# Fused attention and gelu layer on one core: the second layer's products of attentions 2 to 8 in 64x64 form, over four two-bank PSUM tiles

## The chip, the cores and the metric

The kernel runs on one core of a Trainium2 chip. TensorE (PE) does the matrix products and writes them into PSUM, eight banks of 512 float32 values per partition. ScalarE (ACT) does exponentials, gelu and copies, VectorE (DVE) elementwise work, reductions and 32x32 transposes, GpSimd (POOL) elementwise work in SBUF and some DMA issues, SyncE (SP) most DMA issues. Each engine runs its own list of instructions in order, and semaphores connect the lists. The metric is the device time of one execution in microseconds (us), lower is better.

## The reference

For each of 8 batches and 12 heads, with 448 positions and head size 64: q and k are normed by their root mean square and scaled by gains, the scores are a softmax of q times k transposed, and the result is multiplied by v. The heads are then joined to a matrix x of 3584 tokens by 768, and a two-layer network follows.

```python
q_n, k_n = (rmsnorm(q, g_q), rmsnorm(k, g_k))
scores = scale * np.matmul(q_n, k_n.transpose(0, 1, 3, 2))
attn = np.exp(scores - max); attn = attn / sum
x = matmul(attn, v) joined to [3584, 768]
h = x @ w_in                      # 768 x 2048
g = gelu_tanh(h)
out = g @ w_out                   # 2048 x 768
```

## The kernel before, in words

The work goes batch by batch, b = 0 to 7. A batch has an *attention*, a *first layer* (x times w_in, then gelu) and a *second layer* (g times w_out). The program's text is a hand-written order (`manual_schedule`): the instructions of an engine run in the order in which the Python code issues them.

**Attention** (`attention`, and `first_attention` for batch 0). The 12 heads are 3 groups c of 4. A group has 7 *units* t (line 333): four products of 64x64 weights with 448 columns each fill one two-bank PSUM tile `t` with the scores of 64 keys for four heads, and one ACT exponential (line 337) turns them into `ex`. DVE adds the `ex` of a group over t into `es` (`key_sums`, lines 353 to 359). Per group follow the *sums' product* (ones times `es`, four 64x64 products, line 384), the transposes, reciprocal and spreading of the sums on DVE (`turned`, `recips`, lines 393 to 404), the *value products* (v times `ex`, 28 products, line 384), and `quad_x` (line 417), which multiplies both into `xT`. Attention of batch b+1 is interleaved with the second layer of batch b, so that PE has work while ACT does the exponentials. "Attention 2" is that of b = 1.

**First layer**. For each of 16 blocks f of 128 gelu inputs, six 128x128 products of 448 columns go into one PSUM bank or one half of a two-bank tile. Blocks 0 to 3 go through `mm1_pair` (line 482), into two-bank tiles with one gelu of 896 columns (line 487); from block 4 on `mm1` (line 431) uses one bank from the pool `ps_m` and a gelu of 448 columns each (line 437).

**Second layer** (`mm2`, line 452). For a tile i of 128 tokens and a half of the 768 output columns, 16 products of 128x128 weights (a slice of g) with 384 columns of w_out add up in one bank of `ps_m`; then DVE (line 462) or ACT (line 460) copies them to `osb`, and when both halves are there two DMAs store the tile. Batches come in pairs with 7 tiles: 3 after the first, 4 after the second. `m2_parts` lists the products; `attention` gives them out in portions between groups of two or three units (`cuts`, `shares`). For b = 0 the list has all first halves ahead of all second halves (`order.sort`), and w_out itself is loaded in two halves of its columns by POOL's DMA queue (line 663). What is left after batch 7 runs at the end.

**PSUM** is 2 banks of `ps_m` and two-bank tiles that `pair` hands out in turn (`rounds`): two at first, three (`t0` to `t2`) once `start` is closed ahead of attention 2, which frees the banks of the first attention.

**Preparing q and k.** Loads (SP queue), squares (ACT or POOL), sums of squares (DVE reductions, line 170), norming (POOL), transposes by DMA and a gain on DVE (line 320) run ahead for later batches, at places given by the lists `m1`, `side`, `behind` and `ends`. In attention 2, POOL's squares of batch 2 wait for the gain of group 2 of batch 1 (line 673, `gpsimd_waits`), and six reductions on DVE follow them (`behind`, slot 4).

Of the kernel before, what the change touches and what calls it, by code (L numbers as in the profile page):

```python
# [17 lines left out]
def kernel(  # L18
# [43 lines left out]
    ps_m = ctx.enter_context(tc.tile_pool(name="ps_m", bufs=2, space=bass.MemoryType.PSUM))  # L62
    ps_t = ctx.enter_context(tc.tile_pool(name="ps_t", bufs=1, space=bass.MemoryType.PSUM))
    start = ctx.enter_context(ExitStack())
    ps_o = start.enter_context(tc.tile_pool(name="ps_o", bufs=1, space=bass.MemoryType.PSUM))
# [8 lines left out]
    def three():  # L74
        return len(rounds) == 3
# [164 lines left out]
    def rsqrt_last(b):  # L240
# [4 lines left out]
        if three():  # L245
            own, dst = pair("root")[:, 0], y
        else:
            own, dst = oall[0][:, S:], place(b, 1)
# [94 lines left out]
    def key_sums(b, c, t):  # L343

        n = added(b, c)
        if t > n or t == 0:
            return
        ex = exs[b, c]
        if t == 1:
            ess[b, c] = exq.tile([P, 2, S], BF16, tag="es", name="es")  # L350
        es = ess[b, c]
        if t == 1:
            nc.vector.tensor_add(es, ex[:, 0], ex[:, 1])
        elif t == n and n % 2 == 0 or c + 1 == NCH and t > 3:
            nc.vector.tensor_add(es, es, ex[:, t])  # L355
# [12 lines left out]
    def products(b, c, what, lo=0, hi=NT):  # L368

        if lo == 0 and three():  # L370
            o = oas["o", what] = pair("o")
            oas[what] = [o[:, r, :S] for r in range(2)]
        elif lo == 0:
            oas[what] = spare.pop() if spare else [o[:, :S] for o in oall]
        o = oas[what]
        es = [exs[b, c][:, t] for t in range(NT)]
        if not what and added(b, c):
            es[:added(b, c) + 1] = [ess[b, c]]
# [34 lines left out]
    def quad_x(b, c):  # L413
        if c == 0:
            xT[b] = xp.tile([128, HP, S], BF16, tag="xT", name="xT")
        if three():
# [25 lines left out]
    osbs, by_act = {}, []  # L442

    def mm2(b, i, half, f, lo, hi):

        end = b + 1 == B and i + 1 == 2 * S // 128
        if f == 0:
            osbs["ps"] = ps_m.tile([128, 512], F32, tag="mm", name="o")
            if lo == 0:
                osbs[i] = op.tile([128, d_model], F32, tag="osb", name="osb")  # L450
        o, osb = osbs["ps"][:, :hi - lo], osbs[i]
        nc.tensor.matmul(  # L452
            o, g[:, f, i * 128:(i + 1) * 128], wout[:, f, lo:hi],
            start=(f == 0), stop=(f == nf - 1),
        )
        if f + 1 < nf:
            return
        last = end and hi == d_model
        if b + 1 == B and (lo == 0 or end) or by_act:
            nc.scalar.copy(osb[:, lo:hi], o)  # L460
        else:
            nc.vector.tensor_copy(osb[:, lo:hi], o)  # L462
        if half == 0 and not end:
            return
        for j in range(2):
            col = i * 128 + j * R
            r = ((b // 2) * 2 + col // S) * R
            cols = slice(lo if end else 0, hi)
            eng = nc.scalar if last and j else nc.sync
            eng.dma_start(  # L470
                out_v[col % S // R, r:r + R, cols], osb[j * R:(j + 1) * R, cols]
            )

    def mm1_pair(i, cs=range(HP), b=0, js=range(2)):
# [11 lines left out]
        if cs[-1] == HP - 1 and js[-1] == 1:  # L486
            nc.scalar.activation(  # L487
                g[:, 2 * i:2 * i + 2, (b % 2) * S:(b % 2 + 1) * S], h[:, :, :S],
                AF.Gelu_apprx_tanh
            )  # L490

# [4 lines left out]
    def m2_parts(b):  # L496
        tiles = range(3) if b % 2 == 0 else range(3, 7)
        order = [(i, half) for i in tiles for half in range(2)]
        if b == 0:

            order.sort(key=lambda t: t[1])
        parts = [(i, half, half * HD, (half + 1) * HD) for i, half in order]
        if b + 1 == B:
            i, half, lo, hi = parts.pop()
            parts += [(i, half, lo, lo + HD // 2), (i, half, lo + HD // 2, hi)]
        return [
            lambda part=part, f=f: mm2(b, part[0], part[1], f, *part[2:])
            for part in parts for f in range(nf)
        ]

    def attention(b, m2, quota, side, behind, ends):


        units = [(c, t) for c in range(NCH) for t in range(NT)]
        cuts = (0, 3, 6, 9, 11, 13, 16, 18, 21)
        groups = [units[i:j] for i, j in zip(cuts, cuts[1:])]
        first, last, tail = (23, 16, 4) if b > 1 else (20, 14, 3)
        sums_at, x_at = {3: 0, 6: 1}, {4: 0}
        shares = (0, 13, 26, 35, 45, 58, 69) if b > 1 else (0, 13, 26, 34, 40, 53, 59)
        spread = quota - first - last - tail  # L520
        given = 0

        def upto(k):
            nonlocal given
            while given < k:
                m2.pop(0)()
                given += 1

        before = []
        for i, group in enumerate(groups):  # L530
            for fn in side.get(i, ()):
                fn()
            if b == 1 and i == 3:
                by_act.append(b)
            for c, t in group:
                unit(b, c, t)
            for c, t in before:
                key_sums(b, c, t)
            if i in x_at:
                products(b, x_at[i], 1)  # L540
                quad_x(b, x_at[i])
            elif i in sums_at:
                products(b, sums_at[i], 0)
                turned()
            if i == 0:
                n = first
            elif i < len(shares):
                n = spread * shares[i] // shares[-1] - spread * shares[i - 1] // shares[-1]
            else:
                n = last  # L550
            end = given + n

            upto(end - n // 2)
            if i in sums_at:
                recips()
            for c, t in group[:1 if i else 0]:
                key_sums(b, c, t)
            upto(end - n // 4)
            for c, t in group[1 if i else 0:-1]:
                key_sums(b, c, t)  # L560
            upto(end)
            before = group[-1:]
            for fn in behind.get(i, ()):
                fn()
        for fn in ends:
            fn()
        nc.scalar.preload_act_table_set(GELU_SET)

# [3 lines left out]
        c = NCH - 1  # L572
        products(b, c - 1, 1)
        for c, t in before:
            key_sums(b, c, t)
        quad_x(b, c - 1)
        products(b, c, 0)
        turned()
        products(b, c, 1)
        recips()  # L580

        by_act.append(b)
        upto(quota)
        mm1_pair(0, early, b)
        quad_x(b, c)
        mm1_pair(1, early, b)
        by_act.clear()

# [201 lines left out]
    m2 = []  # L790
    for b in range(B):
# [30 lines left out]
        elif b + 1 < B:  # L822

            m1.append((0, lambda: gpsimd_waits(ess[b, NCH - 1][:1, 0, :1])))
# [20 lines left out]
        for f in range(nf // 2 if b == 0 else nf):  # L845
# [8 lines left out]
            elif f > 3:  # L854
                mm1(b, f)
# [49 lines left out]
```

## Time and profile before

| | |
|---|---|
| times shown | 404.07 us median of 3 (403.87 to 404.14) |
| profiled execution: span of its instructions | 402.9 us |
| around the span (median less span) | 1.2 us |
| PE busy, share of the span | 394.0 us, 98% |
| ACT, DVE, POOL busy | 280.8, 257.7, 123.6 us |
| granted PE clock | 9 tenths or more in all 40 slices |
| attention 4 begins, attention 5 begins (PE) | 190.48 us, 237.43 us |

The profiled execution's own time is its span and about 1.2 us around it, so that its 402.9 us stand for the 404.07 us of the median. In a row of a timeline the columns are the start in us, the length in us, the engine, the source line, the operation with what it writes and reads, and the count of merged instructions; in square brackets stands the idle time ahead of it with what ended it. A row of the chain of work has the start, the length, the engine with the written tile and its line, and the count. In a row of the groups the two numbers behind the bar are the busy time in us and the mean of one in ns, then the idle time ahead of them.

### The profile page before, as it was taken

What the parts mean: (1) busy time and instruction counts of PE and PEld (TensorE: products, weight loads), DVE (VectorE), ACT (ScalarE), POOL (GpSimd) and SP (SyncE); (2) the same over time, 40 slices, a digit from 0 to 9 for tenths busy, and PEclk for the clock granted to TensorE, in tenths of its full rate; (3) what the DMA queues carried; (4) which work ended last, traced back from release to release, by engine and by line L of the source; (5) the groups of instructions that cost most, each with busy time, mean ns of one, the idle gap of its engine ahead of it and who ended that gap; (6) DMA issues with size and microseconds to landing.
All of it is one profiled execution on the core that took longest, in us unless ns stands there. A gap on an engine that the chain in (4) does not pass through costs nothing.

```text
span 402.9 us, 8097 instructions
## 1 busy us (share of the span) xinstructions
PE 394.0 (98%) x3319; PEld 209.7 (52%) x3319; DVE 257.7 (64%) x436; ACT 280.8 (70%) x382; POOL 123.6 (31%) x104
## 2 busy tenths in 40 slices
PE   7799999999999999999999999999999999999996
PEld 3365555555555555554555555555555545555564
DVE  5999868975796369845699257963698405990010
ACT  6995498778974887857975789748878359744301
POOL 4993407454007230183004540072301800000000
PEclk9999999999999999999999999999999999999999
DMA  8999996998415964169612948149513511210033
GB/s 287 297 224 207 199 210 215 243 242 222 91 39 116 245 110 131 41 167 279 114 41 63 251 69 217 40 86 266 77 42 78 117 24 39 51 47 23 2 78 80
DMA packets 65577, 54.07 MB, mean 134 GB/s; under 512 B 37380, under 2 KB 60548, under 8 KB 65540
## 3 DMA queue, kind: packets, MB, share of 16 engines
q1 hardware_dynamic: 53184, 41.48, 38.7%
q0 software_dynamic: 12128, 11.80, 19.0%
q8 instruction: 26, 0.43, 0.4%
q10 hardware_dynamic: 228, 0.28, 0.2%
q14 instruction: 11, 0.09, 0.1%
HBM read 45.61 MB, written 11.01 MB: 141 GB/s over the span
## 4 chain that ended last, share of the span: by engine, by line
PE 92%; ACT 4%; DMA 2%; POOL 1%; SPq 0%; DVE 0%; issue 0%
PE o L452 38%; PE h L431 24%; PE t L482 12%; PE t L333 9%; PE t L384 8%; ACT ex L337 4%; DMA rawq<-in_q_dram 2%; POOL g L161 1%; PE tp L291 0%; PE o L384 0%; SPq L626 0%; PE os L384 0%; DVE ss L170 0%; ACT lg L195 0%; SPq L121 0%
## 5 line engine op out<-in xcount | busy, mean ns | idle before, releaser
L337 ACT ACTIVATE ex<-t,shift 128x896 bf16<-128x896 f32 x168 | 157.4, 1006 | 21.7 <-PE t L333 19.3
L452 PE MATMUL o<-wout,g 128*128 128x384 bf16 (+1 forms) x912 | 156.8, 324 | 0.0
L452 PEld LDWEIGHTS <-g 128*128 128x128 bf16 x912 | 83.6, 98 | 67.8 <-issue 18.8
L431 PE MATMUL h<-xT,win 128*128 128x448 bf16 x516 | 99.1, 352 | 0.0
L170 DVE TENSOR_REDUCE ss<-sq 128x14 f32<-128x896 f32 (+3 forms) x45 | 44.3, 999 | 48.9 <-ACT sq L159 45.9
L431 PEld LDWEIGHTS <-win 128*128 128x128 bf16 x516 | 50.5, 98 | 47.1
L437 ACT ACTIVATE g<-h 128x448 bf16<-128x448 f32 x86 | 46.6, 543 | 28.2 <-PE h L431 23.1
L462 DVE COPY osb<-o 128x384 f32<-128x384 f32 x41 | 22.7, 553 | 52.8 <-PE o L452 50.8
L333 PE MATMUL t<-qT,kT 64*64 64x448 bf16 x672 | 47.0, 359 | 2.6 <-ACT lg L195 1.0
L482 PE MATMUL t<-xT,win 128*128 128x448 bf16 x252 | 49.5, 353 | 0.0
L673 POOL COPY mark<-es 1x1 bf16<-1x1 bf16 x6 | 1.1, 176 | 131.8 <-DVE es L355 124.6
L487 ACT ACTIVATE g<-t 128x896 bf16<-128x896 f32 x21 | 18.4, 915 | 32.9 <-PE t L482 32.9
L273 POOL TENSOR_TENSOR nrmq<-rawq,rinv 128x896 bf16<-128x896 f32 (+1 forms) x21 | 34.8, 1658 | 10.0 <-DVE o L236 6.4
L482 PEld LDWEIGHTS <-win 128*128 128x128 bf16 x252 | 24.5, 98 | 22.6 <-issue 0.4
L273 POOL TENSOR_TENSOR nrmk<-rawk,rinv 128x896 bf16<-128x896 f32 x20 | 33.6, 1680 | 0.0
L333 PEld LDWEIGHTS <-kT 64*64 64x64 bf16 x672 | 17.4, 105 | 27.4 <-issue 20.3
L384 PE MATMUL t<-ex,vb 64*64 64x448 bf16 x588 | 31.6, 350 | 0.0
L460 ACT COPY osb<-o 128x384 f32<-128x384 f32 (+1 forms) x16 | 7.3, 458 | 31.4 <-PE o L452 31.4
L404 DVE STREAM_TRANSPOSE rb<-rc 128x896 f32<-128x896 f32 (+1 forms) x25 | 26.8, 1073 | 0.8
L384 PEld LDWEIGHTS <-vb 64*64 64x64 bf16 x672 | 20.2, 107 | 12.0 <-issue 3.0
L358 DVE TENSOR_TENSOR e<-ex 128x896 bf16<-128x896 bf16 x33 | 20.0, 606 | 9.7 <-ACT ex L337 9.4
L393 DVE STREAM_TRANSPOSE st<-t 128x448 f32<-128x448 f32 x42 | 24.6, 624 | 1.0 <-PE t L384 0.9
(93 smaller groups left out, 296.2 us busy)
## 6 DMA issues: line engine op xcount, KB each, us to landing
out_dram<-osb SPq DMA_DIRECT2D x54, 192.0 KB, 2.7
rawq<-in_q_dram SPq DMA_DIRECT2D x23, 448.0 KB, 4.6
rawk<-in_k_dram SPq DMA_DIRECT2D x23, 448.0 KB, 5.8
vb<-in_v_dram POOLq DMA_DIRECT2D x6, 672.0 KB, 6.5
win<-in_moe_w_in_dram POOLq DMA_DIRECT2D x8, 384.0 KB, 10.4
wout<-in_moe_w_out_dram POOLq DMA_DIRECT2D x2, 1536.0 KB, 22.3
vb<-in_v_dram POOLq DMA_DIRECT2D x2, 448.0 KB, 17.9
vb<-in_v_dram POOLq DMA_DIRECT2D x2, 224.0 KB, 12.1
```

Source lines behind the costliest of these rows:

```text
L170: nc.vector.reduce_sum(sss[b][:, seat(b, c), "qk".index(n), hs, ts], squares(b, c, n, hs, ts), axis=AX.X)
L273: eng.tensor_mul(nrms[n, b, c][:, ts].rearrange("p t a d -> p a t d"), raws[n, b, c][:, :, ts], root[:, :, ts].to_broadcast([P, 2, m, D]),)
L333: nc.tensor.matmul(sc[r * R:(r + 1) * R, a, :S], kT[rs, c, t, r], qT[b][rs, c, :, r], start=True, stop=True,)
L337: nc.scalar.activation(ex[:, t], sc[:, :, :S], AF.Exp, scale=scale, bias=shift)
L384: nc.tensor.matmul(o[r][a * D:(a + 1) * D], vb[b % 2][rs, 2 * c + a, i] if what else ones[rs], es[i][rs, a], start=(i == 0), stop=(i == n ...
L393: nc.vector.transpose(st[:, r].rearrange("p a b -> p (a b)"), oas[0][r])
L404: nc.vector.transpose(oas["rb"][:, rs].rearrange("p r s -> p (r s)"), rc.to_broadcast([128, (rs.stop - rs.start) * m, 32]),)
L431: nc.tensor.matmul(h[:, :S], win[:, c, f * 128:(f + 1) * 128], xT[b][:, c], start=(c == 0), stop=(c == HP - 1),)
L437: nc.scalar.activation(g[:, f, (b % 2) * S:(b % 2 + 1) * S], h[:, :S], AF.Gelu_apprx_tanh)
L452: nc.tensor.matmul(o, g[:, f, i * 128:(i + 1) * 128], wout[:, f, lo:hi], start=(f == 0), stop=(f == nf - 1),)
L462: nc.vector.tensor_copy(osb[:, lo:hi], o)
L482: nc.tensor.matmul(h[:, j, :S], win[:, c, f * 128:(f + 1) * 128], xT[b][:, c], start=(c == 0), stop=(c == HP - 1),)
```

## The change

It replaces `mm2`, `m2_parts` and the giving out by portions.

- In attentions 2 to 8 the second layer goes by whole tiles of 128 tokens (`quartered`): a *step* is four products of 64x64 weights with 384 columns, one for each pair of a half r of the 128 inner values of block f and a half a of the tokens. Half r goes to bank `(r + turn) % 2`, that is to that half of the output columns. 16 steps make turn 0, 16 more turn 1, with the banks changed over. Ahead of turn 1 PE waits (`follows`) for the last product of turn 0. The tile sits in one two-bank PSUM tile, which is taken out of the rotation for that time, and one copy of 768 columns brings it out: DVE for the first tile of an attention, ACT for the other two.
- The order in an attention is written out as a list: "u" a unit, a number so many steps, "s" a group's sums' product with `turned` and `recips`, "x" its value products with `quad_x`. Units stand single between 4 to 6 steps. Three tiles (96 steps) go into each attention; from attention 3 on, one more half tile is done in the old form by `whole` behind it.
- `ps_m` is released with `start`, and two more two-bank tiles take those banks: `rounds` has four (`t0` to `t3`). The first layer from block 4 on uses `mm1_pair` with gelus of 896 columns, but the last pair has its two gelus apart.
- `key_sums` adds pairs: `es` has room for two, and the sums of a group are two additions of 1792 columns, a fold of 896 and one more of 896, where there were six of 896.
- The last four tiles (`final`) take a two-bank tile each, both halves in the old form, with a copy for each half.

```diff
+    def quartered(b, i, eng):
+        o = rounds.pop(0)
+        for turn in range(2):
+            for f in range(nf):
+                if turn and f == 0:
+                    follows(mm)
+                for r in range(2):
+                    rs, half = slice(r * D, (r + 1) * D), (r + turn) % 2
+                    for a in range(2):
+                        at = i * 128 + a * R
+                        mm = nc.tensor.matmul(
+                            o[a * R:(a + 1) * R, half, :HD], g[rs, f, at:at + R],
+                            wout[rs, f, half * HD:(half + 1) * HD],
...
+                if turn and f + 1 == nf:
+                    rounds.append(o)
...
+        for what in ("u", 16, "uuu", 6, "u", 5, "u", 5,
+                     4, "u", 5, "u", 5, "u", 2, "us", 5, "u", 5, "u", 5, "u", 1,
+                     5, "uxu", 4, "u", 4, "u", 3, "us", 2, "u", 4, "u", 4, "u", 6, "x", "sx"):
...
+                    elif made > 2:
+                        key_sums(b, *done[-3])
...
+        if b > 1:
+            half, i = b % 2, 6
+            o = pair("o")[:, half, :HD]
+            whole(i, o, half * HD, (half + 1) * HD)
...
-        if t == 1:
-            nc.vector.tensor_add(es, ex[:, 0], ex[:, 1])
-        elif t == n and n % 2 == 0 or c + 1 == NCH and t > 3:
-            nc.vector.tensor_add(es, es, ex[:, t])
-        elif t % 2:
-            e2 = exq.tile([P, 2, S], BF16, tag="e2", name="e2")
-            nc.vector.tensor_add(e2, ex[:, t - 1], ex[:, t])
-            nc.vector.tensor_add(es, es, e2)
+        if t == 3:
+            nc.vector.tensor_add(es, ex[:, :2], ex[:, 2:4])
+        elif t == 5:
+            nc.vector.tensor_add(es, es, ex[:, 4:6])
+            nc.vector.tensor_add(es[:, 0], es[:, 0], es[:, 1])
+        elif t == 6:
+            nc.vector.tensor_add(es[:, 0], es[:, 0], ex[:, 6])
...
-                mm1(b, f)
+            elif f + 1 == nf:
+                mm1_pair(f // 2, b=b, js=(0,))
+                mm1_pair(f // 2, b=b, js=(1,))
+            elif f % 2 and f > 3:
+                mm1_pair(f // 2, b=b)
...
+            for i in (2, 3):
+                rounds.insert(0, ps_x.tile([128, 2, 512], F32, tag=f"t{i}", name=f"t{i}"))
```

More of the change, by code (lines that the diff above doesn't have):

```diff
@@ L441 @@
     out_v = out.rearrange("(r t) d -> t r d", t=NT)
[L442 to L465, printed above, removed]
+    osbs = {}
@@ L466, in mm2, with osb_of, store @@
+    def osb_of(i):
+        osbs[i] = op.tile([128, d_model], F32, tag="osb", name="osb")
+    def store(b, i, lo=0, hi=d_model, engs=(nc.sync, nc.sync)):
+        for j, eng in enumerate(engs):
             col = i * 128 + j * R
             r = ((b // 2) * 2 + col // S) * R
-            cols = slice(lo if end else 0, hi)
-            eng = nc.scalar if last and j else nc.sync
             eng.dma_start(
-                out_v[col % S // R, r:r + R, cols], osb[j * R:(j + 1) * R, cols]
+                out_v[col % S // R, r:r + R, lo:hi], osbs[i][j * R:(j + 1) * R, lo:hi]
@@ L494 @@
     even, odd = early[::2], early[1::2]
[L496 to L509, printed above, removed]
@@ L511, in attention @@
-    def attention(b, m2, quota, side, behind, ends):
-        units = [(c, t) for c in range(NCH) for t in range(NT)]
-        cuts = (0, 3, 6, 9, 11, 13, 16, 18, 21)
[L516 to L565, printed above, removed]
```

145 lines of the change are left out of this document (111 added, 34 removed).

## The prediction

> **What bounds the kernel now.** I read the page's busy shares and the chain that ended last, then that chain in order of time, then the timelines of PE, ACT, DVE and POOL, and the groups of instructions for durations.
>
> ```profile
> PE 394.0 (98%) x3319; PEld 209.7 (52%) x3319; DVE 257.7 (64%) x436; ACT 280.8 (70%) x382; POOL 123.6 (31%) x104
> PE 92%; ACT 4%; DMA 2%; POOL 1%; SPq 0%; DVE 0%; issue 0%
> ```
> ```profile
> 190.55 0.69 PE t L333 x12
> 191.24 3.84 PE o L452 x23
> ...
> 203.67 1.32 PE t L384 x28
> ...
> 215.62 2.97 PE t L384 x60
> ...
> 219.34 4.54 PE t L482 x24
> 223.88 13.62 PE h L431 x72
> 237.50 0.69 PE t L333 x12
> ...
> 378.35 20.85 PE o L452 x144
> ```
>
> PE is the bound, and in attentions 2 to 8 it never waits. The rows give its prices. The last row is 128 full slots (32 of its 144 products have half the columns): 20.85 / 128 = 0.163 us for 384 columns. 13.62 / 72 = 0.189 us for 448 columns. 28 small products are 7 sets of four: 1.32 / 7 = 0.189 us a set, so four 64x64 products side by side take what one 128x128 product takes. A period is 237.50 - 190.55 = 46.95 us. Its work is 45 sets and 96 first-layer products at 0.189 and 112 second-layer products at 0.163, together 44.9. The missing 2.05 us is changes of array form: between 190.55 and 219.34 PE goes nine times into 64x64 products and back, so 0.23 each. From single rows: 0.69 - 3 x 0.189 = 0.12 going in, 3.84 - 23 x 0.163 = 0.09 coming out, 0.21. I take 0.22.
>
> **The change part by part.** All sums are against the profiled execution: span 402.9 us, about 1.2 us around it, together the median of 404.07.
>
> *Removed: changes of form.* The list in `attention` leaves one round trip of nine. 8 x 0.22 x 7 attentions = 12.3 us of PE time. A step is four products of 384 columns; its nearest row is the 0.189 set of 448 columns, and with the columns it comes to 0.163 (bounds: 0.163, and 0.189 if something other than columns set that row; I take 0.163, because 0.189 equals the full-array price of 448 columns exactly). So the second layer itself costs what it did. Whether the 12.3 us come out depends on what is late next, and I find five places.
>
> *1. The second half of w_out.*
>
> ```profile
> L663 POOL DMA_DIRECT2D wout<-in_moe_w_out_dram x2: 1204/1213/1222, 26.8 to 32.0; - x2
> DMA to landing us min/median/max: 18.5/22.3/26.2
> ```
> ```profile
> 50.79 0.76 PE L333 MATMUL t<-qT,kT 64*64 64x448 bf16 x12
> 51.48 3.42 PE L452 MATMUL o<-wout,g 128*128 128x384 bf16 x20
> ...
> 61.35 1.47 PE L452 MATMUL o<-wout,g 128*128 128x384 bf16 x8
> ...
> 78.32 4.70 PE L482 MATMUL t<-xT,win 128*128 128x448 bf16 x24
> ```
>
> The second half is issued at 32.0 and lands 26.2 later, at 58.2. Before, 48 products use first halves only, and the 49th (in the row at 61.35) comes after the landing. After, the first step already has r = 1 writing the second half of the columns: PE stands from its third small product of attention 2 until 58.2, with all units behind it in its list. Against 51.48 that is **6.7 us**. The DMAs ahead of it are unchanged, so its bounds are narrow, 6 to 7.5. (The first unit also waits for the transposes' last copy, whose banks its tile now has; that lies inside the same wait.)
>
> *2. The rest of attention 2.*
>
> ```profile
> 60.18 0.45 DVE L320 TENSOR_SCALAR kT<-kT,gcols 128x896 bf16<-128x896 bf16 x1
> ...
> 64.81 1.09 DVE L417 TENSOR_TENSOR xT<-t,rb 128x896 bf16<-128x896 f32 x1 [0.58 <-PE t L384]
> 65.82 4.17 DVE L170 TENSOR_REDUCE ss<-sq 128x14 f32<-128x896 f32 x6
> ```
> ```profile
> 61.59 1.68 POOL L161 TENSOR_TENSOR sq<-rawq 128x896 f32<-128x896 f32 x1 [0.72 <-DMA rawq<-in_q_dram]
> ...
> 66.65 1.82 POOL L161 TENSOR_TENSOR sq<-rawk 128x448 f32<-128x448 f32 x2
> ```
> ```profile
> rawk<-in_k_dram SPq DMA_DIRECT2D x23, 448.0 KB, 5.8
> ```
>
> Before, `quad_x` of group 0 (64.81) stands ahead of the six reductions. In the new list `behind` is emitted with unit 14, ahead of that `quad_x`. The reductions need POOL's squares, which begin after the gain and take 68.5 - 61.6 = 6.9 us. After, the sums of group 0 are ready about 10.3 us after restart, 68.5, the gain ends at 68.9, the squares at 76.0, the reductions at 76.6, `quad_x` at 77.7. Unit 17 needs the PSUM tile that this `quad_x` reads, and PE is there at about 76.0: a wait of 1.7, or of 2.8 if the loads of groups 1 and 2 (issued at about 67.2 behind two stores, 5.8 to land) hold the squares up by 1.1. I take 2.8 (bounds 1.7 and 3.6). PE's own work from 58.2 is 25.3 us (52 sets, 96 steps, less what ran before); with waits of 0.85 at the first sums' product and 1.2 at the third (reckoned as in 3) and 0.2 in all elsewhere it is 30.35. Before, 78.32 - 51.48 = 26.84: **+3.5 us**, the removed 1.8 of changes included.
>
> *3. Attentions 3 to 8: DVE's sums are late.*
>
> ```profile
> 190.48 0.76 PE L333 MATMUL t<-qT,kT 64*64 64x448 bf16 x12
> ...
> 201.24 0.36 PE L384 MATMUL t<-es,ones 64*64 64x448 bf16 x4
> ...
> 216.90 0.36 PE L384 MATMUL t<-es,ones 64*64 64x448 bf16 x4
> ```
> ```profile
> 192.44 2.80 ACT L337 ACTIVATE ex<-t,shift 128x896 bf16<-128x896 f32 x3
> ```
> ```profile
> 199.67 0.62 DVE L355 TENSOR_TENSOR es<-es,ex 128x896 bf16<-128x896 bf16 x1
> ...
> 201.79 1.17 DVE L393 STREAM_TRANSPOSE st<-t 128x448 f32<-128x448 f32 x2
> 202.99 0.33 DVE L399 RECIPROCAL rc<-st 128x28 f32<-128x28 f32 x1
> 203.36 1.11 DVE L404 STREAM_TRANSPOSE rb<-rc 128x896 f32<-128x896 f32 x1
> ...
> 214.75 2.08 DVE L355 TENSOR_TENSOR es<-es,ex 128x896 bf16<-128x896 bf16 x3
> ```
> ```profile
> L355 DVE TENSOR_TENSOR es<-es,ex 128x896 bf16<-128x896 bf16 x33 | 20.6, 623 | 2.8
> L462 DVE COPY osb<-o 128x384 f32<-128x384 f32 x41 | 22.7, 553 | 52.8 <-PE o L452 50.8 <-DMA out_dram<-osb 1.9
> ```
>
> Before, the first sums end at 200.29, 0.95 ahead of their product; the third end at 216.83, 0.07 ahead of theirs. There is no room at the third. New sizes have no row. The copy of 768 columns: an estimate of 0.95, from 0.553 for 384 and 1.09 for 896. An addition of 1792 columns: 1.08, taking 0.15 of 0.623 as fixed, as the copy's line through those points gives; bounds 0.62 (no dearer than 896) and 1.25 (twice). Dependent DVE rows stand 0.04 apart (202.99 + 0.33 to 203.36), independent ones overlap by 0.08.
>
> With T the first unit: exponentials begin at T + 1.96 and come every 0.9 (2.80 less 1.0 for one, over two). Units 2 to 4 follow 16 steps, so exponentials 2, 3, 4 begin at 3.2, 4.1, 5.0, and the fourth ends at 6.0. DVE: addition to 7.1, copy of the first tile to 8.0, addition to 9.0, fold to 9.65, addition to 10.3. PE is at the first sums' product after 10 units and 48 steps, 9.7: **wait 0.65**. Then 0.19 + 21 steps + 4 units and 0.1 bring value products 0 to 14.8 to 16.15, and 4 units and 11 steps the second sums' product to 18.7. DVE: transposes, reciprocal, spread until 13.5, addition to 14.5, `quad_x` 16.35 to 17.4, addition to 18.45, fold to 19.1, addition to 19.75: **wait 1.1**. Then 0.19, 3 units, 16 steps and value products 1 bring the third to 24.5; DVE has the second spread until 22.9, then two additions, fold and addition until 26.35: **wait 1.9**. From 26.4 follow 0.19 + 1.32 + 0.1 + 16 x 0.163: the first layer begins at T + 30.6. Before it was 219.34 - 190.55 = 28.8. So **+1.8 us** in each of six attentions: waits of 3.65 against 1.8 removed.
>
> *4. The last gelus of a first layer.*
>
> ```profile
> L437 ACT ACTIVATE g<-h 128x448 bf16<-128x448 f32 x86 | 46.6, 543 | 28.2 <-PE h L431 23.1
> L431 PE MATMUL h<-xT,win 128*128 128x448 bf16 x516 | 99.1, 352 | 0.0
> L487 ACT ACTIVATE g<-t 128x896 bf16<-128x896 f32 x21 | 18.4, 915 | 32.9 <-PE t L482 32.9
> L460 ACT COPY osb<-o 128x384 f32<-128x384 f32 (+1 forms) x16 | 7.3, 458 | 31.4 <-PE o L452 31.4
> ```
>
> In the built order the second half of the last pair waits for the gelu of the first half, which reads the same two-bank tile. A result is there 0.352 - 0.189 = 0.163 after its slot; gelu 0.543; two hand-overs at 0.045: **0.8 us**, seven times, 5.6. Before, two banks in turn hid it.
>
> *5. `final`.* In the same way the second half of each of the last four tiles waits for the copy of the first: 0.163 + 0.458 + 0.09 = 0.7, **2.85 us** in all.
>
> *At nothing:* `follows` (two sets or more stand between the turns, 0.38 against 0.163 + 0.05 until the product is done; without that cover 0.2 x 21 = 4); ACT's copies of 768 columns (0.78 by 0.458 and the slope of 0.915 and 0.543; ACT has 21 x 0.9 + 1.6 + 0.7 = 21.2 us in an attention of 30); pairs of gelus in the first layer (0.915 against 12 products, 2.27); stores, as many and as large.
>
> Sum: 6.7 + 3.5 + 6 x 1.8 + 5.6 + 2.85 = 29.5; 402.9 + 29.5 + 1.2 = **433.6 us**.
>
> **The rivals.**
>
> *A. PE works past a waiting product (faster).* If products further down PE's list ran while one waits, only PE's own work would count: 404.07 - 12.3 = 391.8. The waits found above come to 29.5 + 12.3 = 41.8 us; the change is faster only if over 29.5 of them, 7 tenths, are filled so. Against it:
>
> ```profile
> 28.38 0.38 PE L333 MATMUL t<-qT,kT 64*64 64x448 bf16 x4 [0.52 <-ACT ex L337]
> ```
>
> PE stood 0.52 us for an exponential though later products were in its list. Chance 0.04.
>
> *B. Small products are bound by issue.* 28 products with their loads in 1.32 us are 23.6 ns an instruction. If that is a floor, a step takes 0.189: at most 0.026 x 672 = 17.5 us more; waits for DVE swallow about half: 442. The exact equality with the full-array price speaks against it. Chance 0.11.
>
> *C. Weight loads lie bare.*
>
> ```profile
> L384 PEld LDWEIGHTS <-vb 64*64 64x64 bf16 x672 | 20.2, 107 | 12.0 <-issue 3.0
> ```
>
> If each step paid its 0.107 load, 672 x 0.107 = 72: about 506. The 0.189 set contains such loads and shows none of it. Chance 0.02. [...]
>
> *D. Wide additions are cheap.* At 0.62 the waits of 3 fall from 3.65 to about 1.5 and some of attention 2 goes: 420. The row of 623 ns is for half the columns, so this needs columns to cost nothing. Chance 0.07.
>
> **How the numbers follow.** Forecast 0.76, with a range of its own of 427 to 440 (place 2, the additions by 0.08 either way); A 0.04, B 0.11, C 0.02, D 0.07. 0.2% of the time is what a measurement can tell from no change. Faster 0.03 and same 0.01 are A; slower 0.96. The range of 423 to 443 has the forecast, most of B and the dear half of D, and leaves out A, C and the rest.
>
> **What would show it.** A gap on PE in attention 2 that ends near 58.2 by the second w_out load; periods of about 49.5 us; sums' products with waits of 0.65, 1.1 and 1.9 ended by DVE additions; 0.8 ahead of the last half pair, ended by a gelu; four gaps of 0.7 at the end; second-layer steps 0.163 apart. It is wrong if steps are 0.189 or more apart, if additions of 1792 columns are far from 1.08, or if a wait behind `follows` shows.

## The result, and the profile after

The changed kernel takes **440.5 us** (median of 4 runs, 439.65 to 441.2) against 404.07 us (4 runs, 403.87 to 404.14): a ratio of 1.090, with a 95% interval of 1.088 to 1.091. It is slower by 36 us. The prediction said 433.6, with 423 to 443 as its range and 427 to 440 as the forecast's own. The side and the range hold; the point is 6.9 us short.

From the page of the changed kernel: the busy shares and the chain that ended last by engine, which the prediction shows of before, and between them the granted PE clock in 40 slices, where before every slice had 9:

```profile
PE 389.8 (89%) x5335; PEld 236.5 (54%) x5335; DVE 240.4 (55%) x365; ACT 282.6 (64%) x357; POOL 123.4 (28%) x104
...
PEclk9999969999999999999999999999999999999999
...
PE 55%; DVE 17%; DMA 9%; ACT 7%; POOL 6%; issue 5%; SPq 0%; DVEq 0%; ACTq 0%; POOLq 0%
```

PE is busy for 4 us less than before, and its share falls from 98% to 89% of a longer span (438.6 us). The chain goes through PE for 55% where it was 92%: DVE, a DMA, ACT and POOL now release work that PE stands in front of. One slice of 40 has a lower clock, of which more below.

The view of waits on PE, of the changed kernel (engine, tile and line, then who ended the wait: us in total, times, longest):

```profile
PE t L386 <- DVE es L361: 21.6, 18, 1.9
PE t L485 <- DMA wout<-in_moe_w_out_dram: 7.0, 1, 7.0
PE t L509 <- ACT g L516: 4.4, 7, 0.6
PE t L460 <- ACT osb L606: 2.4, 4, 0.6
...
PE t L336 <- DVE xT L419: 1.4, 1, 1.4
...
PE t L336 <- DVE rawk L142: 0.9, 1, 0.9
```

The first five rows are the forecast's five places: DVE's sums 18 times (three in each of six attentions), the second half of w_out once, the last gelu seven times, `final` four times, and a unit in attention 2. Together they are 36.8 us of idle PE. The last row is the first unit of attention 2, of which more at the end of the part on the prediction. The view counts idle time only, from the end of the product ahead, which lies behind the end of that product's slot (0.35 us against 0.189 for 448 columns), so a start-to-start gap is 0.16 to 0.20 longer than its row in attention 4 (0.74 for 0.57, 2.09 for 1.93).

The timeline of PE in attention 4 of the changed kernel (the attention begins at 159.78 and the next at 210.00, a period of 50.22 where it was 46.95):

```profile
160.00 2.77 PE L485 MATMUL t<-wout,g 64*64 64x384 bf16 x64
162.60 0.74 PE L336 MATMUL t<-qT,kT 64*64 64x448 bf16 x12
...
170.24 0.38 PE L386 MATMUL t<-es,ones 64*64 64x448 bf16 x4 [0.57 <-DVE es L361]
...
179.90 0.38 PE L386 MATMUL t<-es,ones 64*64 64x448 bf16 x4 [1.09 <-DVE es L361]
...
186.70 0.38 PE L386 MATMUL t<-es,ones 64*64 64x448 bf16 x4 [1.93 <-DVE es L361]
...
190.95 17.19 PE L509 MATMUL t<-xT,win 128*128 128x448 bf16 x90
208.77 1.29 PE L509 MATMUL t<-xT,win 128*128 128x448 bf16 x6 [0.63 <-ACT g L516]
```

The first row answers rival B: 16 steps take 162.60 - 160.00 = 2.60 us, 0.1625 a step, which is the price of a 128x128 product of 384 columns. The second layer itself got no dearer. In brackets stand the waits for the three sums, and the last row is the half pair that waits for a gelu. As start-to-start gaps they are 0.74, 1.29, 2.09 and 0.80. Without these four gaps a period would be 45.30 us, 1.65 less than the 46.95 of before.

The DVE timeline of the same attention shows why the third is the longest:

```profile
181.98 1.11 DVE L406 STREAM_TRANSPOSE rb<-rc 128x896 f32<-128x896 f32 x1
183.02 1.05 DVE L356 TENSOR_TENSOR es<-ex 128x1792 bf16<-128x1792 bf16 x1
184.17 1.09 DVE L358 TENSOR_TENSOR es<-es,ex 128x1792 bf16<-128x1792 bf16 x1
185.29 0.62 DVE L359 TENSOR_TENSOR es<-es 128x896 bf16<-128x896 bf16 x1
186.02 0.62 DVE L361 TENSOR_TENSOR es<-es,ex 128x896 bf16<-128x896 bf16 x1
```

DVE is not idle here: the third group's four additions begin only as the second group's spread (L406) ends, at 183.1, and they end at 186.64. PE has been out of work since 184.8. DVE is busy for 55% of the span and is nevertheless what PE waits for.

The second half of w_out, in the PE timeline of the changed kernel, and the windows around its landing (busy us of PE, PEld, DVE, ACT and POOL with counts, the granted clock, the DMA share, GB/s):

```profile
50.81 0.55 PE L294 MATMUL tp<-ident,nrmk 128*128 128x128 bf16 x7
52.28 0.38 PE L336 MATMUL t<-qT,kT 64*64 64x448 bf16 x4 [0.92 <-DVE rawk L142]
52.47 0.35 PE L485 MATMUL t<-wout,g 64*64 64x384 bf16 x2
59.85 4.09 PE L485 MATMUL t<-wout,g 64*64 64x384 bf16 x62 [7.03 <-DMA wout<-in_moe_w_out_dram]
```
```profile
54.00:56.00 2.00, 0.00 (x0) 0.00 (x0) 0.00 (x0) 0.00 (x0) 0.00 (x0) 0.93 1.27 192
56.00:58.00 2.00, 0.00 (x0) 0.00 (x0) 0.00 (x0) 0.00 (x0) 0.00 (x0) 0.50 1.21 254
...
59.80:61.00 1.20, 1.15 (x16) 0.87 (x19) 0.00 (x0) 0.00 (x0) 0.00 (x0) 0.50 0.98 262
61.00:62.40 1.40, 1.40 (x24) 0.95 (x17) 0.00 (x0) 0.00 (x0) 0.00 (x0) 0.50 0.55 117
62.40:63.60 1.20, 1.20 (x33) 1.01 (x29) 0.00 (x0) 0.00 (x0) 0.00 (x0) 0.94 0.02 3
```

PE stands from its second small product until 59.85, as the forecast had it. What it did not have is the clock: while PE idled, the grant fell to 0.50, and it stayed there after the data had come. From the shares of the first and the last window it was at half from 55.7 to 62.5, so that the first 2.7 us of work ran at half speed. The 62 products are 15.5 steps, 2.52 us at 0.1625, and the next unit begins 3.77 us after their start, at 63.62, so the half clock lost 1.25 us.

Where the 35.7 us between the two spans lie: up to the first layer of attention 2, +12.2; the first layer of attention 2, +0.8; five periods (attentions 3 to 7) by 3.27, +16.4; the last attention with its layer and `final`, +6.4. The remaining 0.7 of the 36.4 is not in the kernels. The 1.2 us that were put around the span of before set one execution's span against the median of others; where time and span of one and the same execution are known, they are 2.0 us apart before (404.84 and 402.8) and 2.1 after (440.73 and 438.6).

### The profile page after: what moved, and what is told of

Read it like the earlier page. It is cut to its first block, busy times and chain, and to the rows that moved or that the text cites. A ratio compares the mean times of both kernels' runs of the same rounds, so it can differ in the third digit from the quotient of the medians.

```text
span 438.6 us, 12084 instructions
## 1 busy us (share of the span) xinstructions
PE 389.8 (89%) x5335; PEld 236.5 (54%) x5335; DVE 240.4 (55%) x365; ACT 282.6 (64%) x357; POOL 123.4 (28%) x104
## 4 chain that ended last, share of the span: by engine, by line
PE 55%; DVE 17%; DMA 9%; ACT 7%; POOL 6%; issue 5%; SPq 0%; DVEq 0%; ACTq 0%; POOLq 0%
PE t L509 29%; PE t L485 9%; PE t L460 9%; DMA wout<-in_moe_w_out_dram 6%; PE t L386 6%; ACT ex L340 5%; DVE es L358 5%; DVE es L359 3%; DMA rawq<-in_q_dram 3%; DVE es L361 3%; PE t L336 2%; POOL g L164 2%; DVE xT L419 2%; DVE st L395 2%; POOL sq L164 2%
## 5 line engine op out<-in xcount | busy, mean ns | idle before, releaser
L509 PE MATMUL t<-xT,win 128*128 128x448 bf16 x756 | 145.9, 352 | 4.4 <-ACT g L516 4.4
L485 PE MATMUL t<-wout,g 64*64 64x384 bf16 x2688 | 133.1, 325 | 7.0 <-DMA wout<-in_moe_w_out_dram 7.0
L516 ACT ACTIVATE g<-t 128x896 bf16<-128x896 f32 (+1 forms) x70 | 58.1, 842 | 73.2 <-PE t L509 73.2
L485 PEld LDWEIGHTS <-g 64*64 64x64 bf16 x2688 | 83.8, 108 | 36.3 <-issue 7.4
L336 PE MATMUL t<-qT,kT 64*64 64x448 bf16 x672 | 60.2, 352 | 5.0 <-DVE xT L419 1.4
L356 DVE TENSOR_TENSOR es<-ex 128x1792 bf16<-128x1792 bf16 x20 | 21.3, 1065 | 52.0 <-ACT ex L340 52.0
L460 PE MATMUL t<-wout,g 128*128 128x384 bf16 (+1 forms) x240 | 38.3, 315 | 2.4 <-ACT osb L606 2.4
L460 PEld LDWEIGHTS <-g 128*128 128x128 bf16 x240 | 22.5, 98 | 18.1 <-issue 5.5
L419 DVE TENSOR_TENSOR xT<-t,rb 128x896 bf16<-128x896 f32 x21 | 22.8, 1088 | 12.5 <-ACT ex L340 11.7
L406 DVE STREAM_TRANSPOSE rb<-rc 128x896 f32<-128x896 f32 (+1 forms) x25 | 26.8, 1073 | 0.8
L164 POOL TENSOR_TENSOR sq<-rawq 128x896 f32<-128x896 f32 (+1 forms) x9 | 13.6, 1511 | 38.1 <-DVE ss L173 35.0
```

The lines of the kernel that those rows point to most:

```text
L164: eng.tensor_mul(sq, raw, raw)
L336: nc.tensor.matmul(sc[r * R:(r + 1) * R, a, :S], kT[rs, c, t, r], qT[b][rs, c, :, r], start=True, stop=True,)
L419: nc.vector.tensor_mul(xT[b][:, 2 * c:2 * c + 2], oas["o", 1][:, :, :S], oas["rb"])
L460: nc.tensor.matmul(o, g[:, f, i * 128:(i + 1) * 128], wout[:, f, lo:hi], start=(f == 0), stop=(f == nf - 1),)
L485: mm = nc.tensor.matmul(o[a * R:(a + 1) * R, half, :HD], g[rs, f, at:at + R], wout[rs, f, half * HD:(half + 1) * HD], start=(turn == 0 and ...
L509: nc.tensor.matmul(h[:, j, :S], win[:, c, f * 128:(f + 1) * 128], xT[b][:, c], start=(c == 0), stop=(c == HP - 1),)
```

## The experiments

The theory was that PE's own work became cheaper by the changes of form, and that five places where PE now stands idle took that back and more. The rivals were that some of the idle time would return elsewhere as soon as it is taken away at one place, that the second layer in 64x64 is itself dear, and that the changes of form had cost nothing in the first place. The ratios below are to the kernel before on the same chip, with the 95% interval in brackets.

### One place at a time

**Attention 2 with its second layer in the old form** (places 1 and 2): its three tiles in 128x128, first halves of all tiles first, with the order of units that the kernel before has there.

```diff
...
+        if b == 1:
+            m2 = halved(b - 1, tiles)
...
+        early_list = ("uuu", 20, "uuu", 13, "uuu", 13, "uus", 8, "uux", 6, "uuu", 13, "uus", 6, "uuu", 17, "x", "sx")
-        for what in ("u", 16, "uuu", 6, ...
+        for what in early_list if b == 1 else ("u", 16, "uuu", 6, ...
```

> Attention 2 alone is put back: its second layer in 128x128 products, first halves of all tiles ahead of second halves, units in groups of two and three as before; all else as in the changed kernel. Theory (the second half of w_out holds PE up, and the DVE and POOL waits of that attention are a cause of their own): the wait of 7.0 us and the slow clock behind it (about 1.2) go, eight form changes (1.8) come back, the waits for reductions and sums stay: attention 2 from 57.3 to about 50.5, in all 433.5 us. Rival 1 (those other waits only follow from the late start): attention 2 back to 45.8, in all 429. Rival 2 (not w_out but the rotation of four tiles or the wide sums make attention 2 long): over 438.

Measured: 432.8 us, 1.070 [1.066, 1.074]. Attention 2 takes 50.24 us where it took 57.28, and the other periods stay at 50.22. The PE timeline has no wait for w_out any more, and shorter ones in its place:

```profile
72.55 1.52 PE L386 MATMUL t<-ex,ones 64*64 64x448 bf16 x28 [1.59 <-ACT osb L542]
...
81.02 0.38 PE L386 MATMUL t<-es,ones 64*64 64x448 bf16 x4 [0.86 <-DVE es L359]
```

The theory's number holds. Attention 2 is still 4.5 us longer than the 45.78 of before, and the gelu's wait (0.8) and these are most of it. The first row waits for ACT's copy of second-layer halves, which sit in one of the four rotating tiles where they used to have banks of their own; the second waits for DVE's sums. The granted clock is 1.00 throughout, so in these runs the half clock goes with the wait for w_out.

**The last pair of the first layer in two tiles** (place 4):

```diff
-        if cs[0] == 0 and js[0] == 0:
+        if cs[0] == 0 and (js[0] == 0 or len(js) == 1):
             hs1[i] = pair("hh")
```

> The two halves of the last first-layer pair go to two different two-bank tiles, so that the second need not wait for the gelu of the first. Theory: 0.80 us less in each of seven batches, 440.5 - 5.6 = 434.9 us, and the gap ahead of those six products is gone. Rival (the wait only moves: the first exponential of the next attention or the first unit's tile is late instead): 440 to 441.

Measured: 436.3 us, 1.079 [1.074, 1.083]. The first layer is one row again in the timeline:

```profile
190.76 18.32 PE L509 MATMUL t<-xT,win 128*128 128x448 bf16 x96
```

The periods are 49.43, shorter by the expected 0.79. The total fell by 4.2 and not by 5.6: in this run w_out landed at 60.0, and the clock was at half until 64.3 (up to 62.5 in the changed kernel), which took back about 0.8, and the unit that waits for the first `quad_x` stood 1.9 us in the view of waits instead of 1.4.

**The second halves of the last four tiles in another tile** (place 5):

```diff
-                    po = (pair("o")[:, 0] if lo > HD else o[:, half])[:, :hi - lo]
+                    po = (pair("o")[:, 0] if lo > 0 else o[:, half])[:, :hi - lo]
```

> The second halves of the last four tiles go to another two-bank tile than the first halves. Theory: four waits of 0.75 go, 440.5 - 3.0 = 437.5 us. Rival (the end is set by the copies and stores, not by PE): 440 to 440.5.

Measured: 438.5 us, 1.084 [1.079, 1.089]; the stretch from the last attention's first unit to the end is 75.76 us where it was 77.96, so 2.2 less, and the four gaps are gone. The direction holds, the size is three quarters of the forecast's. PE's products there take 21.0 us again as before; but from the end of PE's last product to the end of the span it is 4.7 us, where the changed kernel has 3.8. So 0.9 came back behind PE's last product.

**DVE without the fold and the last addition** (place 3; the sums' product on TensorE takes three sets instead of one):

```diff
-            es[:added(b, c) + 1] = [ess[b, c][:, 0]]
+            es[:min(added(b, c), 5) + 1] = [ess[b, c][:, 0], ess[b, c][:, 1]]
...
             nc.vector.tensor_add(es, es, ex[:, 4:6])
-            nc.vector.tensor_add(es[:, 0], es[:, 0], es[:, 1])
-        elif t == 6:
-            nc.vector.tensor_add(es[:, 0], es[:, 0], ex[:, 6])
```

> DVE leaves out the fold and the last addition of a group's sums; the sums' product takes three sets of four small products (two rows of es and the last ex) where it took one. PE gets 6 sets of 0.189 more in an attention, 1.13 us. Theory (DVE's chain of additions, reciprocal and quad_x sets the pace of an attention): the waits ahead of the three sums' products fall from 0.74, 1.25 and 2.09 to about 0, 0 and 0.6; 2.3 us less in each of six attentions, a little less in attention 2: 427 us. Rival (PE or ACT set the pace and the waits would turn up elsewhere): 440.5 + 7 = 447 us.

Measured: 425.65 and 432.09 us, two runs too far apart for an interval; the periods of the profiled execution are what counts. They are 48.26, then 47.90: 2.3 shorter, as expected, although PE has six more sets in each. The timeline of attention 4 shows one wait left of three:

```profile
180.46 0.57 PE L383 MATMUL t<-es,ones 64*64 64x448 bf16 x8 [0.54 <-DVE es L358]
```

The rival, that DVE's time does not matter because PE would be bound by its own six extra sets, is out.

**`whole` ahead of the third sums** (place 3, without taking work from DVE): the 16 products in 128x128 that stood behind the third value products go between the second value products and the third sums, which costs PE one more round trip between the forms.

```diff
-                     ..., "u", 4, "u", 4, "u", 6, "x", "sx"):
+                     ..., "u", 4, "u", 4, "u", 6, "x", "wsx"):
...
+                elif w == "w":
+                    if b > 1:
+                        seventh()
...
```

> The changed kernel, with the score products that run in 128x128 (`whole`) moved ahead of the third sums' product in attentions 3 to 8, so that TensorE has work while the third addition of DVE ends. Theory (the third sums' wait of 1.9 us is time in which TensorE has nothing else to do): the wait goes, and one more change of form at 0.22 us comes, so some 1.5 us fewer in each period, about 48.7 us, and 430.5 us in all. Rival (DVE is only pushed further: the wait returns at a later product): periods stay at 50.2 us and the time at 440.

The expectation calls the products of `whole` score products; they are of the second layer, g times w_out.

Measured: 430.0 us, 1.063 [1.058, 1.067], periods of 48.32. The timeline and the waits:

```profile
182.84 2.77 PE L460 MATMUL t<-wout,g 128*128 128x384 bf16 x16
185.54 0.38 PE L386 MATMUL t<-es,ones 64*64 64x448 bf16 x4
185.75 1.49 PE L386 MATMUL t<-ex,vb 64*64 64x448 bf16 x28
```
```profile
PE t L386 <- DVE es L361: 10.0, 12, 1.1
```

The third sums' product follows without a gap, and the row that had 18 waits has 12. A period fell by 1.9, which is the gap of 2.09 less a round trip of 0.2. The wait did not come back at a later product. In attention 2 of this run the clock was at half for 10.2 us instead of 6.8, and it took 58.40 where it took 57.28. The gain is not touched by it, since w_out landed 0.9 earlier (58.96), and attention 3 begins at 109.59, as in the changed kernel (109.56).

**w_out's second half issued right behind the first** (place 1, where the issue stands):

```diff
-            lambda: w_out_part(0), lambda: load_v(1, 0, 2),
+            lambda: w_out_part(0), lambda: w_out_part(1), lambda: load_v(1, 0, 2),
...
-            lambda: w_out_part(1), lambda: load_v(1, 2, 4)),
+            lambda: load_v(1, 2, 4)),
```

> The changed kernel with the second half of w_out issued right behind the first half, instead of behind the loads of v and the squares of attention 1. Theory (the 16 DMA engines are busy with what was issued before, so the landing is set by the bytes ahead and not by the issue): it lands 1 to 2 us earlier, and the time falls by 1 to 2 us, to about 439. Rival (the landing follows the issue by a fixed time): it lands 4 us or more earlier, and the time falls to 436 or less.

Measured: 438.7 us, 1.084 [1.080, 1.089]. Issued at 28.7 instead of 32.5, it landed 28.7 later instead of 27.3: at 57.4, so 2.4 us earlier, between the two theories' landings. The time fell by 1.8 only:

```profile
57.42 4.94 PE L485 MATMUL t<-wout,g 64*64 64x384 bf16 x62 [4.46 <-DMA wout<-in_moe_w_out_dram]
```
```profile
57.40:61.50 4.10, 4.08 (x52) 2.92 (x55) 0.00 (x0) 0.00 (x0) 0.00 (x0) 0.50 1.00 266
```

PE starts earlier, but the clock comes back at about 61.8, so it works at half speed for 4.4 us instead of 2.7. Of the 2.4 us won, 0.85 go there, and attention 3 begins 1.5 us earlier (108.07). Whether the bytes ahead or a fixed time set the landing is not settled by this run.

### Is the removed term real?

**The kernel before with 13 more round trips per attention**: one second-layer product between the units of each group. No engine has more work.

```diff
-            for c, t in group:
+            base = given
+            for k, (c, t) in enumerate(group):
+                if k:
+                    upto(given + 1)
                 unit(b, c, t)
...
-            end = given + n
+            end = base + n
```

> The kernel before, with one product of the second layer between the units of each group, so that the form of the products changes 13 more round trips in each of attentions 2 to 8; the amount of work on every engine is that of the kernel before. Theory (a round trip between the 128x128 and the 64x64 form costs TensorE 0.22 us): 7 x 13 x 0.22 = 20 us more, about 424 us, and the period of an attention 46.95 + 2.9 = 49.8 us. Rival (the change of form is hidden, and what the first kernel gained from its groups is something else): 404 to 407 us.

Measured: 424.9 us, 1.050 [1.046, 1.054], with periods of 49.94. Here is one of those products between two units:

```profile
198.78 0.38 PE L333 MATMUL t<-qT,kT 64*64 64x448 bf16 x4
199.09 0.34 PE L452 MATMUL o<-wout,g 128*128 128x384 bf16 x1
199.36 0.38 PE L333 MATMUL t<-qT,kT 64*64 64x448 bf16 x4
```

From unit to unit there are 0.58 us (199.36 - 198.78), of which the set takes 0.189 and the product 0.163; the other 0.23 are the change of form and back. A period is 2.99 longer, 0.230 for each of 13. So the rival that forms cost nothing is out, and at this price the 12.3 us that the forecast took off were there to be had (8 x 0.230 x 7 = 12.9). What the changed kernel itself shows is 1.65 a period, 0.21 for each of eight.

### All places together

**Combined**: the gelus and `final` in other tiles, `whole` ahead of the third sums, the additions one unit earlier, the first sums' product one chunk of steps later, attention 2 in the old form, and its reductions in slot 5.

```diff
-                     ... "u", 2, "us", 5, "u", 5, "u", 5, "u", 1,
-                     ..., "u", 6, "x", "sx"):
+                     ... "u", 2, "u", 5, "us", 5, "u", 5, "u", 1,
+                     ..., "u", 6, "x", "wsx"):
...
-                    elif made > 2:
-                        key_sums(b, *done[-3])
+                    elif made > 1:
+                        key_sums(b, *done[-2])
```

> All that takes a wait away, together: the last first-layer pair in two tiles, the final's second halves in another tile, the score products in 128x128 ahead of the third sums, the sums of the keys one unit earlier, the first sums' product one chunk later, the reductions one slot later, and attention 2 with its second layer in 128x128. Theory (the five places of waits are what made the changed kernel slower, and the form changes saved, 0.22 us each, are real): periods of 46.1 to 46.9 us against 46.95 in the kernel before, 401 to 407 us in all. Rival (something else than the waits makes the 64x64 second layer dear): periods stay over 48 us, and the time over 415.

Measured: 404.9 us, 1.0006 [0.9992, 1.0019]; periods of 46.30 (the first 46.66). It is level with the kernel before: what the periods win, attention 2 gives back (48.6 against 45.78, and it begins 1.2 us later). The additions one unit earlier and the later first sums were not run by themselves.

Two more kernels remove what DVE's order still cost in that one: the fold is emitted with the last addition, and the second and third pair of halves in attention 2 are copied by ACT. The two edits were not run apart. The kernels differ in the slot of attention 2's reductions.

```diff
         elif t == 5:
             nc.vector.tensor_add(es, es, ex[:, 4:6])
-            nc.vector.tensor_add(es[:, 0], es[:, 0], es[:, 1])
+            if n == 5:
+                nc.vector.tensor_add(es[:, 0], es[:, 0], es[:, 1])
         elif t == 6:
+            nc.vector.tensor_add(es[:, 0], es[:, 0], es[:, 1])
             nc.vector.tensor_add(es[:, 0], es[:, 0], ex[:, 6])
...
-                            eng = nc.scalar.copy if k2 and half2 else nc.vector.tensor_copy
+                            eng = nc.scalar.copy if half2 or two[1][1] else nc.vector.tensor_copy
```

> The combined kernel (v11_combined) with three more edits: DVE's fold of the key sums emitted with the last addition, so that xT of the first chunk's product no longer stands behind it; in attention 2 the copies of the second and third pair of output halves on ACT, so that DVE's additions don't wait behind a copy; and the reductions of attention 2 back in slot 4. Theory (the waits of 0.4 to 0.9 us that are left are DVE's order): attentions 3 to 8 at 46.0 us against 46.3, attention 2 one to two us shorter than its 48.6, 401 to 403 us in all, under the first kernel by 0.4 to 0.9%. Rival (what is left is not DVE's order): 404.5 to 405.5, as v11_combined.

> As w2_combined_late_fold, with the reductions of attention 2 in slot 5, as v11_combined had them. Theory (with its second layer back in 128x128, attention 2 gains nothing from the later slot): within 0.5 us of w2_combined_late_fold. Rival (the reductions in slot 4 stand in the way of the transposed sums there): 1 us or more below it.

Measured: 401.3 us, 0.9915 [0.9900, 0.9931], and 401.0 us, 0.9911 [0.9896, 0.9926]. The slot makes no difference (0.35 us). **Both beat the kernel before by 0.9%.** From the page and the PE timeline of the second:

```profile
PE 388.5 (97%) x5047; PEld 228.9 (57%) x5047; DVE 241.7 (61%) x366; ACT 280.7 (70%) x359; POOL 123.5 (31%) x104
```
```profile
162.72 0.39 PE L336 MATMUL t<-qT,kT 64*64 64x448 bf16 x4
163.22 0.38 PE L388 MATMUL t<-es,ones 64*64 64x448 bf16 x4
...
166.60 1.49 PE L388 MATMUL t<-ex,vb 64*64 64x448 bf16 x28
168.03 2.77 PE L462 MATMUL t<-wout,g 128*128 128x384 bf16 x16
170.73 0.38 PE L388 MATMUL t<-es,ones 64*64 64x448 bf16 x4
170.95 1.49 PE L388 MATMUL t<-ex,vb 64*64 64x448 bf16 x28
172.37 18.33 PE L511 MATMUL t<-xT,win 128*128 128x448 bf16 x96
190.64 0.38 PE L336 MATMUL t<-qT,kT 64*64 64x448 bf16 x4
```

From attention 3 on, the view of waits on PE is empty, the period is 45.87, and PE is at 97% of a span of 398.9 us. With one round trip more than the changed kernel it has seven fewer than before, 1.6 us by the measured price; 1.1 of them arrive. Of the 0.5 that do not, 0.3 stand in the first two rows, too short for the view: the unit takes 0.19, but the second sums' product comes 0.50 after it, when DVE's last addition has ended (163.16):

```profile
162.54 0.62 DVE L363 TENSOR_TENSOR es<-es,ex 128x896 bf16<-128x896 bf16 x1
```

Attention 2 (47.51) still gives back 1.7 us of what six periods win.

## Why the prediction was right, and where it was short

**What bounds the kernel, and the removed term: right.** A change of form and back costs 0.23 us in the kernel with 13 more, against 0.22 taken, and the steps take 0.1625, as taken; in the changed kernel 1.65 us a period came out where 1.76 was forecast. Rival B (0.189 a step) is out by the rows of 160.00 and 162.60. Rival C is out by the same rows: a step has four loads, and the groups of the changed kernel put one at 0.108, so bare loads would show. Rival A is out: 36.8 us of waits are idle time, and no product further down the list ran in them. Rival D is out: the two additions of 1792 columns took 1.065 and 1.086 on average, against the 1.08 estimated (the line that the prediction draws gives 1.10 when it is worked out), and DVE's copy of 768 columns took 0.95, as estimated.

**Place 1, the second half of w_out: mechanism right, mis-sized.** 6.7 was forecast, counted from 51.48; it was 8.4. The landing was taken over from the trace of before, as 58.2; in the changed kernel's profile the load was issued 0.5 later and took 27.3 instead of 26.2, so that it landed at 59.8, and in the other runs with this order between 58.2 and 60.0. The bounds of 6 to 7.5 were too narrow, because the forecast held that DMAs whose order does not change land when they did.

**Place 2, the rest of attention 2: near, by errors that cancel, so by luck.** From the restart to the first layer, 30.35 was forecast, and it took 90.51 - 59.85 = 30.66. The unit behind the first `quad_x` waited as forecast, but the gap is 1.6 (1.41 in the view) instead of 2.8: POOL's squares ran from 72.01 to 78.87 without a gap, so the loads did not hold them up, and 1.7, the value without that delay, was the one to take. The third sums' product waited 0.45 in the view instead of 1.2. Against that, the half clock, which no step had, cost 1.25, and the value products ahead have a gap of 0.4 for which the view names no engine.

**Place 3, DVE's sums: right, and short by 0.67 us a period.** The waits are 0.74, 1.29 and 2.09 where 0.65, 1.1 and 1.9 were worked out, each longer by a tenth or two. Up to the first layer it is +2.5 us in each attention instead of +1.8, some 4 us over six: 0.47 of the 0.67 are the waits, and 0.15 are the changes of form, of which 1.65 came out instead of 1.8. Of the terms of the sum this is the one that was most off in total. The two experiments on it (the sums on TensorE, `whole` ahead) move the period by what the waits say.

**Place 4, the gelus: right.** 0.80 forecast and measured; undone, the periods fall by 0.79. The hand-overs of 0.045, for which the prediction shows no row, come out too (the chain of before has 0.04 from the end of an exponential to the product at 28.38): the half gelu ends at 208.72, and the products behind it begin at 208.77.

**Place 5, `final`: right.** 2.85 forecast, +3.1 measured from the last first layer to the end; undone, 2.2 come back, and the stretch behind PE's last product is 0.9 longer in that run.

**At nothing:** `follows` and ACT's copies of 768 columns (0.79 on average) show no wait, as argued.

So of the 6.9 us that were missing, about 2.0 are places 1 and 2 together (12.2 against 10.2), 4 are place 3, 0.25 place 5, and 0.7 the 1.2 us around the span, which are about 2 in both kernels.

One cost stands in the prediction only as a remark in brackets: the first unit of attention 2 now waits for the transposes' last copy. In the timelines of PE before, of PE after (shown above with the wait for w_out) and of DVE after:

```profile
50.30 0.55 PE L291 MATMUL tp<-ident,nrmk 128*128 128x128 bf16 x7
50.79 0.76 PE L333 MATMUL t<-qT,kT 64*64 64x448 bf16 x12
```
```profile
51.56 0.68 DVE L303 TENSOR_SCALAR kT<-tp,gcols 128x896 bf16<-128x896 bf16 x1
```

Before (and in the kernel with 13 more round trips), the first unit begins 0.49 us after the start of the last transposes, and in all ten kernels with four two-bank tiles 1.47 us after them, with a wait of 0.92. It begins as DVE's last copy out of the transposes' banks ends (52.24 after). The view names a DVE row of 0.06 us that ends together with that copy; that the banks are the cause follows from the kernel's text and the times, and no run takes it apart. In the changed kernel this 1 us is hidden in the wait for w_out, as the prediction says, but in the kernels with attention 2 in its old form it is not. Attention 2 begins at 51.2 to 53.5 in the ten, against 50.79; what is left of the difference is how early the transposes themselves come, from 0.6 us earlier to 1.75 later than before.

## What to carry to other kernels

A round trip between array forms cost 0.23 us where more were put in, and most of that came back where they were taken out. But when the bounding engine got less to do, consumers that had been just in time became late, the third sums' product by 2.09 us: before counting the gain, list for each product what must be ready at its new place, above all where the slack was under 0.1 us (the third sums had 0.07). In this kernel two halves in one tile put the reader of the first half in front of the writer of the second; another tile for the second half gave back 0.8 us a time in the first layer. Single repairs gave 2 to 15 us each. Only several of them together, with DVE's work reordered and the one bad place left in its old form, turned 9% slower into 0.9% faster; the sums on TensorE and the earlier load of w_out are not among them.

## What the runs showed of the hardware that was not expected

In this case the wait for w_out, of 4.2 to 7.2 us on PE, cost more than itself. In the changed kernel the granted clock was 0.50 from 55.7 to 62.5, so 6.8 us, beginning 2.9 us after PE ran dry. It was 6.8 us in four more runs with this wait, beginning 2 to 4 us after PE ran dry and with landings from 57.4 to 60.0, and 10.2 us in one (`whole` ahead: 53.3 to 63.5, beginning 1.6 us after PE ran dry). In the runs where attention 2 has its old form there is no such dip: the granted clock was 1.00 there from 52 to 66 us. What sets the beginning and the length of the halved stretch was not shown.

The price of this wait varied with the place in the halved stretch at which the data came. With the same 6.8 us in both runs, the 62 products behind it lost 1.25 us in the changed kernel, where the data came 4.1 us after the clock fell, and 2.26 us in the run with `final` in other tiles, where it came 2.1 us after. In the run with the earlier load of w_out it came 2.4 us after, and they lost 2.10, so 0.85 more than in the changed kernel. This is most of why moving the load forward by 2.4 us brought attention 3 forward by only 1.5.
